# Sliding-window attention and a SiLU layer on one core: a planner is given later eviction times, and scores and values are placed by new gates

## The chip, the cores and the metric

The kernel runs on one core of one Trainium2 chip, in one launch. The metric is device microseconds of one execution. Six executions of the kernel before took 298.91 to 300.97 us, with a median of 299.58 us.

## The reference

The inputs are q, k and v of shape (8 batches, 8 heads, 576 positions, 64) and two weight matrices, all float32; the output is 4608 x 512 float32.

```python
scores = q @ k.T / 8                       # per batch and head, 576 x 576
mask   = (rel >= 0) & (rel < 64)           # rel = query position - key position
attn   = softmax(where(mask, scores, -1e9))
x      = (attn @ v), heads side by side    # 4608 rows, 512 columns
h      = x @ w_in                          # 512 -> 2048
out    = (h * sigmoid(h)) @ w_out          # 2048 -> 512
```

## The kernel before

**Two kinds of work.** Attention goes batch by batch, in units of three blocks of 64 positions: units (b, 0), (b, 1), (b, 2) for batch b. The dense part goes by tiles of 512 rows, tile 0 to tile 8. Tile b needs the attention of batches up to b. The program adds them in the order batch 0, tile 0, batch 1, tile 1, batch 2, and so on, so that the attention of batch b is meant to be mixed into tile b-1.

**A unit of attention** (from batch 1 on: all 8 heads). *Scores*: 48 small matmuls on a 32-row tiling of TensorE (line 331) into four PSUM banks at0 to at3. *Exponentials*: four on ScalarE (line 337), one per bank. *Masks*: four multiplications on VectorE (line 340). *Values*: 48 small matmuls on a 32-column tiling (line 349) into two banks. Then VectorE takes two reciprocals (356), two multiplications (359) and two transposes (363) into `bridge`, which the dense part reads.

**A dense tile.** First layer: 16 groups of four matmuls 128x512 (line 369), each group into one bank, then a SiLU on ScalarE from that bank (line 375). Second layer: four runs of 16 matmuls 128x512 (line 381), each run into one bank, then a copy (line 387) and a store. A tile from the second on has 64 matmuls in each layer (tile 1's first layer is cut finer; the last run of tile 8 is cut in three).

**Banks.** Eight PSUM banks: 0 to 3 are for scores (pool "at"), 4 to 7 for the dense part (pool "mp"); values take banks 4 and 5 (pool "pv").

**The planner.** Class `Plan` plays the whole program through with a cost for each operation, and the order that comes out is the order of the instructions on every engine. An engine that is free takes, of the operations at the heads of the queues of its classes, the one with the lowest `first` (rank of the class plus batch number), if its dependencies are `done`, its gate is open and its banks are idle. The values of batch b have rank 0 + b, scores 1 + b, a dense matmul 99, SiLU -3, copy-out -2, exponentials and masks 1 + b, reciprocals and the operations after them 0 + b, block transposes and shifts of later inputs 2 + b. An operation counts as done at `seen`, its end plus `lat`, by default 0.08. A bank is idle when the operation that empties it is done. Of idle banks, a dense operation takes first those that values don't use (6 and 7), and of these the one idle longest:

```python
idle.sort(key=lambda i: (op["pool"] == "mp" and i in self.pools["pv"],
                         max([u["seen"] for u in self.banks[i]], default=0.0)))
```

If an operation of another pool than "mp" is ready and only its banks are missing, its pool is kept for it (`kept`). ScalarE keeps one table loaded; a change between exponential and SiLU adds 1.28 in the plan.

The plan's costs, in its own microseconds: a dense matmul of 512 columns 0.0036 + 512/2400 = 0.217 (`lat` 0.1), SiLU of 512 columns 0.605, copy-out on ScalarE 0.621, scores 0.55, values 0.54, an exponential 0.39 (`lat` 0.2), a mask 0.37 (`lat` 0.2).

**Gates.** The list `moe` holds the dense matmuls in order, each with its kind (1: first layer, 2: second) and, for the second layer, `rest`: how many matmuls of the tile's second layer are left. `scores_may_run(whole)` (`whole` is true from batch 1 on) looks at the next dense matmul: scores run only in a second layer, while more than 14 matmuls are left. Values have no gate. Scores also depend on the masks of the unit ahead from batch 2 on (`g_mask[-1]`), on the transposed q and k (`kq_done`) and on the values of three units earlier (`old`).

Of the kernel before, what the change touches and what calls it, by code (L numbers as in the profile page):

```python
# [14 lines left out]
class Plan:  # L15
# [31 lines left out]
    def run(self):  # L47
        head = {c: 0 for c in self.queues}
        engines = sorted({e for q in self.queues.values() for op in q for e in op["us"]})
        free = {e: 0.0 for e in engines}  # L50
        can = {e: [c for c, q in self.queues.items() if any(e in op["us"] for op in q)] for e in engines}
        table, left = "exp", self.count
        pipe, sent = {True: 2.0, False: 0.0}, []
        events, order = [0.0], []
        while left:
            if not events:
                raise RuntimeError([(c, head[c], q[head[c]]["n"]) for c, q in self.queues.items() if head[c] < len(q)])
            now = self.now = heapq.heappop(events)
            while events and events[0] == now:
                heapq.heappop(events)  # L60
            moved = True
            while moved:
                moved = False
                for e in engines:
                    if free[e] > now:
                        continue
                    best, kept = None, set()
                    heads = [(self.queues[c][head[c]], c) for c in can[e] if head[c] < len(self.queues[c])]
                    for op, c in sorted(heads, key=lambda x: x[0]["first"]):
                        if e == "POOL" and op["dma"] and len(sent) >= 8 and sent[-8] > now:  # L70
                            continue
                        if e not in op["us"] or not self.done(op["deps"]) or (op["gate"] and not op["gate"]()):
                            continue
                        if op["pool"]:
                            idle = [i for i in self.pools[op["pool"]] if i not in kept and self.done(self.banks[i])]
                            if len(idle) < len(op["untils"]):
                                if op["pool"] != "mp":
                                    kept.update(self.pools[op["pool"]])
                                continue
                            idle.sort(key=lambda i: (op["pool"] == "mp" and i in self.pools["pv"],  # L80
                                                     max([u["seen"] for u in self.banks[i]], default=0.0)))
                            op["bank"] = idle[:len(op["untils"])]
                            for i, until in zip(op["bank"], op["untils"]):
                                self.banks[i] = until
                        best = (op, c)
                        break
                    if best is None:
                        continue
                    op, c = best
                    head[c] += 1  # L90
                    us = op["us"][e]
                    if op["table"] and op["table"] != table:
                        table, us = op["table"], us + 1.28
                    end = free[e] = now + us
                    soft = e == "POOL"
                    if op["dma"] is None:
                        op["seen"] = end + op["lat"]
                    elif soft:

                        begin = max(pipe[True], end + 1.4)  # L100
                        pipe[True] = begin + op["dma"] * (1.5 if pipe[False] > begin else 1.0)
                        op["seen"] = pipe[True] + op["lat"] + 1.2
                        sent.append(op["seen"])
                        heapq.heappush(events, op["seen"])
                    else:
                        begin = max(pipe[False], end + 1.0)
                        busy = pipe[True] > begin
                        pipe[False] = begin + op["dma"] * (1.6 if busy else 1.0)
                        if busy:
                            pipe[True] += 0.6 * op["dma"]  # L110
                        op["seen"] = pipe[False] + {"ld0": 1.2, "st": 1.2}.get(c, 3.0)
                    op["at"], op["cls"], op["by"] = now, c, e
                    order.append((op, e))
                    left -= c != "warm"
                    moved = True
                    heapq.heappush(events, end)
                    heapq.heappush(events, op["seen"])
        for op, e in order:
            op["fn"](e)
# [3 lines left out]
def kernel(ctx, tc, q, k, v, w_in, w_out, out):  # L123
# [275 lines left out]
    moe = []  # L399
    exps = {}  # L400

    def scores_may_run(whole):
        i = next((i for i in range(scores_may_run.i, len(moe)) if moe[i][0]["seen"] is None), None)
        if i is None:
            return True
        scores_may_run.i = i
        op, kind, rest = moe[i]
        if kind == 1:
            return not whole and rest > 0 and not p.done(op["deps"])
        return rest > (14 if whole else 6)  # L410
    scores_may_run.i = 0

    n_nat = [0, 0]
    def add_first_batch():
# [71 lines left out]
    def add_unit(b, g, which, n0):  # L486
        whole = b > 0
        first = "0" if b == 0 and g == 0 else ""
        na = len(which)
        ns = [n0 + i for i in range(na)]  # L490
        old = [d for n in ns for d in g_pv[n - NE // 2:n - NE // 2 + 1] * (n >= NE // 2)]
        s = p.add("s" + first, {"PE": 0.55 if b else 0.7}, None,
                  [d for a in which for d in kq_done[(b, a)]] + old + (g_mask[-1] if b > 1 else [] if b else c_bias),
                  lat=0.1, gate=lambda: scores_may_run(whole), pool="at" if b else "all", b=b, nb=2 * na)
        s["fn"] = lambda _: scores(s, b, g) if b else scores_first(s, which[0], g)
        s_last[b] = [s]
        ready = []
        for i in range(2 * na):
            ex = p.add("exp" + first, {"ACT": 0.39}, lambda _, i=i: expo(s["bank"][i], 2 * n0 + i), [s], lat=0.2, table="exp", b=b)
            s["untils"][i].append(ex)  # L500
            exps.setdefault(b, []).append(ex)
            if b:
                ex = p.add("mask", {"DVE": 0.37}, lambda _, i=i: masking(2 * n0 + i, g), [ex, *c_mask], b=b)
            ready.append(ex)
        g_mask.append(ready)
        pv = p.add("pv" + first, {"PE": 0.1 + 0.22 * na}, None, ready + [d for a in which for d in v_done[(b, a)]], lat=0.1,
                   pool="pv" if b > 1 or (b, g) > (1, 0) else "at" if b else "all", b=b, nb=na)

        def run_values(_):
            for i, a in enumerate(which):  # L510
                values(pv["bank"][i], b, a, g, ns[i])
        pv["fn"] = run_values
        pv_last[b] = [pv]
        for i, (n, a) in enumerate(zip(ns, which)):
            rc = p.add("inverse" + first, {"DVE": 0.21}, lambda _, i=i, n=n: inverse(pv["bank"][i], n),
                       [pv] + g_norm[n - NRC:n - NRC + 1] * (n >= NRC), b=b)
            no = p.add("norm" + first, {"DVE": 0.56}, lambda _, i=i, n=n: normal(pv["bank"][i], n),
                       [rc] + g_bridge[n - NOX:n - NOX + 1] * (n >= NOX), b=b)
            pv["untils"][i].append(no)
            g_norm.append(no)  # L520
            g_pv.append(pv)
            br = p.add("bridge" + first, {"DVE": 0.5}, lambda _, n=n, a=a: to_bridge(n, b, a, g), [no], b=b)
            g_bridge.append(br)
            o_done.setdefault(NG * b + g, []).append(br)

    n_gt, free_gt = [0], {}
    n_ot, free_ot = [0], {}
# [3 lines left out]
    def add_tile(j):  # L531
# [18 lines left out]
        for i, (ft, lo, hi) in enumerate(work):  # L550
# [3 lines left out]
            for c in range(NDC):  # L554
# [4 lines left out]
                op["fn"] = lambda _, bank=bank, ft=ft, c=c, lo=lo, hi=hi: first_layer(bank, j, ft, c, lo, hi)  # L559
                moe.append((op, 1, 1 if c == 0 and (i == 0 or hi > work[i - 1][2]) else -1))  # L560
            si.append(p.add("silu", {"ACT": 0.18 + (hi - lo) * 0.00083}, lambda _, bank=bank, g=g, lo=lo, hi=hi:
                            silu(bank, g, lo, hi), [op] + free_gt.get(g, []), table="silu"))
            bank["untils"][0] = [si[-1]]
        order = [(m, f, 0, d_model) for m in range(4) for f in range(NFT)]
        if j == 0:
# [4 lines left out]
        for i, (m, f, lo, hi) in enumerate(order):  # L570
# [7 lines left out]
            if f == NFT - 1:  # L578
# [1 line left out]
                n_ot[0] += 1  # L580
                cp = p.add("out", {"DVE": 0.18 + (hi - lo) / 1000, "ACT": 0.18 + (hi - lo) / 1160},
                           lambda e, bank=bank[(m, lo)], ot=ot, lo=lo, hi=hi: copy_out(e, bank, ot, lo, hi),
                           [op, free_ot.get(ot)])
                bank[(m, lo)]["untils"][0] = [cp]
                free_ot[ot] = p.add("st", {"SP": 0.45}, lambda _, ot=ot, m=m, lo=lo, hi=hi: store(ot, j, m, lo, hi), [cp],
                                    dma=0.75 * (hi - lo) / d_model)
# [65 lines left out]
```

The softmax here doesn't subtract the row's maximum and nothing guards it: scores larger than these inputs give would overflow.

## Time and profile before

| | |
|---|---|
| median of six executions | 299.58 us |
| lowest and highest | 298.91 and 300.97 us |
| profiled execution, its own time | 300.97 us |
| its span, first to last instruction | 299.2 us |
| TensorE (PE) busy | 290.7 us, 97% |
| ScalarE (ACT) busy | 176.3 us, 59% |
| VectorE (DVE) busy | 138.8 us, 46% |
| DMA-issuing GpSimd (POOL) | 117.5 us, 39% |
| granted TensorE clock, mean | 1.000 |

Times of the profile are microseconds from the start of the span. A row of the timeline names start, duration, engine, line, operation and count; what stands in brackets is the idle time of the engine before it and what ended that. The duration of one matmul includes the time through the array, so the distance between starts, not the duration, is what one matmul costs TensorE.

### The profile page before, as it was taken

The numbers are of one execution on the slowest core, as the hardware profiler recorded it, in microseconds if no ns is written. First come the engines' busy times: TensorE is split into PE (matmuls) and PEld (weight loads), VectorE is DVE, ScalarE is ACT, GpSimd is POOL, SyncE is SP. The second block draws the span as 40 slices with busy tenths as digits, with TensorE's granted clock in tenths as the row PEclk, the third lists the DMA queues.
The fourth block names the chain that finished last, engine by engine and source line by source line (L and its number), as shares of the span: only waits on it lengthen the run. The fifth ranks groups of instructions, "written<-read, shape, count | busy, mean of one in ns | idle before, by whom it ended". The sixth has DMA issues, their size and how long they took to land.

```text
span 299.2 us, 8516 instructions
## 1 busy us (share of the span) xinstructions
PE 290.7 (97%) x3641; PEld 149.4 (50%) x3641; DVE 138.8 (46%) x340; ACT 176.3 (59%) x340; POOL 117.5 (39%) x175
## 2 busy tenths in 40 slices
PE   7989989899999999999999999999999999999996
PEld 3556635785444544445444544445444544444444
DVE  3682467978886379337941693067006510000000
ACT  4778645886466745675378437752866376126511
POOL 8967976969799979870500000000000000000000
DMA  7999999999999999992860110011001100110012
GB/s 156 175 202 169 148 174 149 228 135 134 172 172 143 112 184 168 154 96 74 82 71 0 72 39 36 2 37 72 35 0 39 72 35 0 37 71 35 2 70 71
DMA packets 82982, 28.64 MB, mean 96 GB/s; under 512 B 72448, under 2 KB 78208, under 8 KB 82944
## 3 DMA queue, kind: packets, MB, share of 16 engines
q0 software_dynamic: 77184, 18.07, 65.5%
q1 hardware_dynamic: 5760, 10.03, 9.4%
q8 instruction: 28, 0.46, 0.7%
q14 instruction: 10, 0.08, 0.1%
HBM read 36.70 MB, written 9.44 MB: 154 GB/s over the span
## 4 chain that ended last, share of the span: by engine, by line
PE 83%; DMA 8%; POOL 6%; issue 1%; ACT 1%; POOLq 0%; ACTq 0%
PE mp L381 40%; PE mp L369 37%; PE at L331 3%; PE mp L349 3%; DMA w_in_sb<-in_moe_w_in_dram 3%; DMA w_out_sb<-in_moe_w_out_dram 2%; DMA vv<-in_v_dram 2%; POOL nat L239 2%; POOL vv L253 2%; POOL natb L229 1%; POOL w_out_sb L265 1%; POOL w_in_sb L259 0%; ACT ot L387 0%; ACT g L375 0%; PE at L349 0%
## 5 line engine op out<-in xcount | busy, mean ns | idle before, releaser
L381 PE MATMUL mp<-w_out_sb,g 128*128 128x512 bf16 (+2 forms) x608 | 130.1, 368 | 1.3 <-DMA w_out_sb<-in_moe_w_out_dram 1.3
L369 PE MATMUL mp<-bridge,w_in_sb 128*128 128x512 bf16 (+5 forms) x696 | 128.9, 342 | 1.6 <-ACT g L375 1.0
L375 ACT ACTIVATE g<-mp 128x512 bf16<-128x512 f32 (+5 forms) x174 | 89.5, 523 | 31.1 <-PE mp L369 29.9
L369 PEld LDWEIGHTS <-w_in_sb 128*128 128x128 bf16 x696 | 66.3, 97 | 62.5 <-issue 7.6
L381 PEld LDWEIGHTS <-g 128*128 128x128 bf16 x608 | 55.9, 98 | 62.6 <-issue 2.0
L387 ACT COPY ot<-mp 128x512 f32<-128x512 f32 (+2 forms) x36 | 20.2, 563 | 62.1 <-PE mp L381 46.2
L340 DVE TENSOR_TENSOR e<-e,mask 128x384 bf16<-128x384 bf16 x84 | 26.0, 347 | 49.3 <-ACT e L337 48.8
L337 ACT ACTIVATE e<-at 128x384 bf16<-128x384 f32 x90 | 37.3, 497 | 16.2 <-PE at L331 15.9
L239 POOL DMA_DIRECT2D nat<-in_k_dram x56 | 34.7, 637 | 11.3 <-DMA vv<-in_v_dram 6.2
L253 POOL DMA_DIRECT2D vv<-in_v_dram x32 | 32.0, 1022 | 12.9 <-PE mp L349 12.5
L239 POOL DMA_DIRECT2D nat<-in_q_dram x56 | 34.8, 641 | 4.0 <-DMA vv<-in_v_dram 1.1
L363 DVE STREAM_TRANSPOSE bridge<-ox 128x384 bf16<-128x384 bf16 x48 | 24.7, 551 | 0.0
L246 DVE STREAM_TRANSPOSE kt<-nat 128x576 bf16<-128x576 bf16 x28 | 20.7, 780 | 6.2 <-DMA nat<-in_k_dram 6.2
L246 DVE STREAM_TRANSPOSE qt<-nat 128x576 bf16<-128x576 bf16 x28 | 20.8, 786 | 3.5 <-DMA nat<-in_q_dram 3.4
L359 DVE TENSOR_TENSOR ox<-mp,rc 128x384 bf16<-128x384 f32 x43 | 21.4, 536 | 0.1
L356 DVE RECIPROCAL rc<-mp 128x6 f32<-128x6 f32 x43 | 7.9, 190 | 18.8 <-PE mp L349 18.0
L349 PEld LDWEIGHTS <-e 128*32 128x32 bf16 x1152 | 10.9, 95 | 9.6 <-issue 5.9
L299 DVE COPY vv<-vv 64x576 bf16<-64x576 bf16 (+1 forms) x14 | 7.4, 530 | 14.2 <-DMA vv<-in_v_dram 11.8
L349 PE MATMUL mp<-vv,e 128*32 128x65 bf16 x1032 | 12.7, 194 | 0.7 <-issue 0.7
L331 PE MATMUL at<-qt,kt 32*128 32x64 bf16 x1008 | 11.6, 190 | 0.0
L331 PEld LDWEIGHTS <-kt 32*128 32x128 bf16 x1008 | 9.3, 92 | 4.3 <-issue 3.3
L337 ACT ACT_TABLE_LOAD x7 | 9.0, 1283 | 0.1
(53 smaller groups left out, 84.7 us busy)
## 6 DMA issues: line engine op xcount, KB each, us to landing
out_dram<-ot SPq DMA_DIRECT2D x35, 256.0 KB, 2.2
vv<-in_v_dram POOLq DMA_DIRECT2D x32, 144.0 KB, 5.4
nat<-in_q_dram POOLq DMA_DIRECT2D x56, 72.0 KB, 4.0
nat<-in_k_dram POOLq DMA_DIRECT2D x56, 72.0 KB, 3.9
w_out_sb<-in_moe_w_out_dram POOLq DMA_DIRECT2D x8, 256.0 KB, 7.0
w_in_sb<-in_moe_w_in_dram POOLq DMA_DIRECT2D x6, 256.0 KB, 7.6
w_in_sb<-in_moe_w_in_dram POOLq DMA_DIRECT2D x4, 128.0 KB, 6.2
natb<-in_q_dram POOLq DMA_DIRECT2D x3, 144.0 KB, 5.9
```

The costliest lines, as they stand in the source:

```text
L239: nc.gpsimd.dma_start(out=nats[i][32 * h:32 * h + 32].rearrange("p (m x) -> p m x", m=NB), in_=(q, k)[kk][b, 4 * a + h].rearrange("(m p r) ...
L246: nc.vector.transpose(out=to[:, (2 * a + part) * S:(2 * a + part + 1) * S].rearrange("x (m t r) -> x m r t", t=32, r=2), in_=nats[i].rearr ...
L253: queue[e].dma_start(out=vv[b % NV][:, 2 * g0 + 1:2 * g1 + 1:2, 0:D], in_=v[b].rearrange("h s d -> (h s) d").rearrange("(g p) d -> p g d", ...
L331: nc.tensor.matmul(at_six(op["bank"][h])[:, a, x], lhsT=kt[b % NK][r, at:at + 128], rhs=qt[b % NK][r, at:at + 64], start=(s == a == x == 0 ...
L337: nc.scalar.activation(out=es[n % NE], in_=at_six(bank), func=ACTF.Exp, scale=scale)
L340: nc.vector.tensor_mul(es[n % NE], es[n % NE], mask0 if g == 0 else mask)
L349: nc.tensor.matmul(at_pv(bank)[32 * h:32 * h + 32, x, t], lhsT=e_of(b, a, n, h)[:, x, 32 * t:32 * t + 32], rhs=vv[b % NV][:, (4 * a + h) * ...
L359: nc.vector.tensor_mul(oxs[n % NOX], at_pv(bank)[:, :, :, 0:D], rcs[n % NRC].unsqueeze(3).to_broadcast([128, 3, 2, D]))
L363: nc.vector.transpose(out=bridge[:, n0:n0 + 3, 2 * a:2 * a + 2].rearrange("x t s (u i) -> x t s u i", u=2), in_=oxs[n % NOX].rearrange("p ...
L369: nc.tensor.matmul(banks[bank["bank"][0]][:, 0:hi - lo], lhsT=w_in_sb[:, c, ft * 128:(ft + 1) * 128], rhs=bridge[:, (j * TT + lo) // 64:(j ...
L375: nc.scalar.activation(out=gts[gt][:, lo:hi], in_=banks[bank["bank"][0]][:, 0:hi - lo], func=ACTF.Silu)
L381: nc.tensor.matmul(banks[bank["bank"][0]][:, 0:hi - lo], lhsT=gts[gt][:, m * 128:(m + 1) * 128], rhs=w_out_sb[:, f, lo:hi], start=(f == 0) ...
```

## The change

Four edits.

1. The `lat` of a SiLU and of a copy-out goes from 0.08 to 0.22 in tiles from the third on (`j > 1`), so that the plan takes their banks to be idle 0.14 later.
2. When all values are placed, the dense part may use all eight banks.
3. Values from batch 2 on get a gate, `values_may_run`: they run when the next scores could run too, or when fewer than five matmuls of the second layer are left, or when the next dense matmul isn't ready, or when no scores are left.
4. Scores from batch 3 on don't run while values are ready and waiting (`values_wait`), and the first scores of a batch (`g == 0`, from batch 3 on) need only more than 3 matmuls left in the second layer, where the others need more than 14.

```diff
                         if op["pool"]:
-                            idle = [i for i in self.pools[op["pool"]] if i not in kept and self.done(self.banks[i])]
+                            idle = [i for i in self.pools[op["pool"] if head["pv"] < len(self.queues["pv"]) else "all"] if i not in kept and self.done(self.banks[i])]
...
-    def scores_may_run(whole):
+    def scores_may_run(whole, more):
...
         if kind == 1:
             return not whole and rest > 0 and not p.done(op["deps"])
-        return rest > (14 if whole else 6)
+        return rest > (more if whole else 6)
     scores_may_run.i = 0
+
+    def next_of(ops):
+        return next((op for op in ops if op["seen"] is None), None)
+
+    def values_wait(b):
+        pv = next_of(p.queues["pv"])
+        return b > 2 and pv is not None and p.done(pv["deps"])
+
+    def values_may_run():
+        s, op = next_of(p.queues["s"]), next_of(op for op, _, _ in moe[scores_may_run.i:])
+        if s is None or op is None or not p.done(op["deps"]):
+            return True
+        kind, rest = next((kind, rest) for o, kind, rest in moe[scores_may_run.i:] if o is op)
+        return kind == 2 and rest < 5 or p.done(s["deps"]) and scores_may_run(True, s["more"])
...
+        more = 3 if b > 2 and g == 0 else 14
         s = p.add("s" + first, {"PE": 0.55 if b else 0.7}, None,
...
-                  lat=0.1, gate=lambda: scores_may_run(whole), pool="at" if b else "all", b=b, nb=2 * na)
+                  lat=0.1, gate=lambda: scores_may_run(whole, more) and not values_wait(b), pool="at" if b else "all", b=b, nb=2 * na)
+        s["more"] = more
...
         pv = p.add("pv" + first, {"PE": 0.1 + 0.22 * na}, None, ready + [d for a in which for d in v_done[(b, a)]], lat=0.1,
+                   gate=values_may_run if b > 1 else None,
...
             si.append(p.add("silu", {"ACT": 0.18 + (hi - lo) * 0.00083}, lambda _, bank=bank, g=g, lo=lo, hi=hi:
-                            silu(bank, g, lo, hi), [op] + free_gt.get(g, []), table="silu"))
+                            silu(bank, g, lo, hi), [op] + free_gt.get(g, []), lat=0.22 if j > 1 else 0.08, table="silu"))
...
-                           [op, free_ot.get(ot)])
+                           [op, free_ot.get(ot)], lat=0.22 if j > 1 else 0.08)
```

## The prediction

> **What bounds the kernel now.** I read the page's busy times first, then TensorE's timeline, then the chain that ended last, then ScalarE's timeline in a first layer, then the windows.
>
> ```profile
> PE 290.7 (97%) x3641; PEld 149.4 (50%) x3641; DVE 138.8 (46%) x340; ACT 176.3 (59%) x340; POOL 117.5 (39%) x175
> ```
>
> TensorE is busy 290.7 of 299.2 us. A gain must come out of its own stream: fewer interruptions, or the few tens of nanoseconds that a busy share doesn't show. Tile 5's second layer on TensorE, from the timeline:
>
> ```profile
> 192.18 0.55 PE L331 MATMUL at<-qt,kt 32*128 32x64 bf16 x48
> 192.66 4.06 PE L381 MATMUL mp<-w_out_sb,g 128*128 128x512 bf16 x18
> 196.65 0.56 PE L349 MATMUL mp<-vv,e 128*32 128x65 bf16 x48
> 197.14 0.55 PE L331 MATMUL at<-qt,kt 32*128 32x64 bf16 x48
> 197.62 4.06 PE L381 MATMUL mp<-w_out_sb,g 128*128 128x512 bf16 x18
> ...
> 206.57 0.56 PE L349 MATMUL mp<-vv,e 128*32 128x65 bf16 x48
> 207.06 2.33 PE L381 MATMUL mp<-w_out_sb,g 128*128 128x512 bf16 x10
> 209.23 14.16 PE L369 MATMUL mp<-bridge,w_in_sb 128*128 128x512 bf16 x64
> 223.32 0.55 PE L331 MATMUL at<-qt,kt 32*128 32x64 bf16 x48
> ```
>
> The pattern of a tile is: scores alone, 18 matmuls, values and scores together, 18, values and scores, 18, values alone, 10, then 64 of the first layer. Tiles 2 to 6 all read so; tile 1 has 21, 21, 21 and 1. The chain's end shows the two layers without attention:
>
> ```profile
> 240.54 14.00 PE mp L369 x64
> 254.53 13.81 PE mp L381 x64
> 268.35 14.08 PE mp L369 x64
> ```
>
> Both layers have 64 matmuls of 512 columns, yet the first takes 0.19 and 0.27 us more. ScalarE's timeline in tile 7's first layer says why:
>
> ```profile
> 247.55 0.60 ACT L375 ACTIVATE g<-mp 128x512 bf16<-128x512 f32 x1 [0.27 <-PE mp L369]
> 248.42 0.60 ACT L375 ACTIVATE g<-mp 128x512 bf16<-128x512 f32 x1 [0.27 <-PE mp L369]
> 249.32 0.60 ACT L375 ACTIVATE g<-mp 128x512 bf16<-128x512 f32 x1 [0.31 <-PE mp L369]
> 250.19 0.60 ACT L375 ACTIVATE g<-mp 128x512 bf16<-128x512 f32 x1 [0.27 <-PE mp L369]
> 251.09 0.60 ACT L375 ACTIVATE g<-mp 128x512 bf16<-128x512 f32 x1 [0.31 <-PE mp L369]
> ```
>
> ScalarE waits for TensorE before each SiLU, so it isn't the bound; but from 248 us on, every second group comes 0.90 instead of 0.87 after the one before. In the plan, ScalarE that has caught up starts a SiLU 0.1 after its group's end; the bank is seen idle at 0.1 + 0.605 + 0.08 = 0.785, before the next-but-one group at 4 x 0.217 = 0.868. So the plan swings between banks 6 and 7 only. On the chip the bank comes back later: its return ends the period of the delayed group, 0.863 (13.81/16) plus some 0.044, so about 0.907 after the group's end. Every second group stalls TensorE for 0.044 us, since the stall itself gives the other bank time. While ScalarE lags (table load, then four SiLUs in a row) the plan itself goes on to banks 4 and 5, and no stall shows.
>
> **Edit 1, banks by later eviction times.** With `lat` 0.22 the bank is seen idle at 0.925, after 0.868; the plan must take a third bank (4 or 5) every third group, and a bank then has two groups' time, 1.73 us on the chip against the 0.907 it needs. The rotation ends the stall. Worth: tile 7 0.19, tile 8 0.27; in tiles 2 to 6 a first layer lasts 14.09 (209.23 to 223.32), of which 0.095 is the switch to small tiles worked out below, so 0.185 over 13.81. Sum 5 x 0.185 + 0.19 + 0.27 = **1.39 us**, all on the path, as TensorE never waits for data there. Bounds: nothing (the plan finds no third bank) to 1.39. I take the whole: the nearest row is tile 1's first layer, which already rotates over three or four banks (shorter SiLUs against shorter groups), and whose long run shows no such stall. SiLUs, copies and stores issue the same DMAs on SP; nothing is queued anew.
>
> The page "TensorE: Matmul & The Clock Gate", section "A second HAM failure mode: psum-queue depth-cycling", speaks against this edit: by it, 512-column matmuls that cycle through banks leave micro-idles that make the clock fall to half and recover. By that rule one of the page's windows of 3.4 us at half clock would cost 1.7 us, an estimate from that page alone, and the sum would be no gain. The windows of the trace stand against it here, PEclk being the third number from the end:
>
> ```profile
> 84.62:98.70 14.08, 14.08 (x65) 6.12 (x63) 9.84 (x16) 10.61 (x17) 13.48 (x20) 1.00 1.65 145
> 268.18:282.26 14.08, 14.08 (x65) 6.19 (x64) 0.00 (x0) 9.54 (x16) 0.00 (x0) 1.00 0.05 19
> ```
>
> The clock is 1.00 in both, the first over its early groups on four banks, the second on two with the stalls.
>
> **Edit 2, all banks after the last values.** It touches tiles 7 and 8 and the end of 6; there it makes the third bank certain. No further gain; its part is in the 1.39.
>
> **Edits 3 and 4, where scores and values stand.** What a place costs: 64 second-layer matmuls take 13.81, 0.2158 each, so 18 take 3.885; from 192.66 to 196.65 they take 3.99. The 0.105 over is the turn to the small tiling at the end (about 0.095) and the restart (about 0.01). Scores cost 0.48 (192.18 to 192.66) and values 0.49 whether a dense matmul or scores follow (206.57 to 207.06, 196.65 to 197.14). Values and scores side by side therefore save one 0.105.
>
> How many pairs come about, by the plan. Tile 1 stays: values (2, 2) come at 1 left, and fewer than five open the gate. Tile 2: scores at 64, pairs at 46 and 28, values (3, 2) at 10; the next scores (4, 0) now need only more than 3, their q and k are transposed in tile 2's first layer, so they go beside: a pair gained. The values (4, 0) become ready in tile 3's first layer and wait there some 10 us for the second. Behind them on TensorE nothing waits, for the plan puts first-layer matmuls there instead; their reader is tile 4's first layer, 27 us on; the masked `es` buffers and rows they hold are asked for three units later. Tile 3: pair (values (4, 0), scores (4, 1)) at 64, pairs at 46 and 28, the last with scores (5, 0). Values (5, 0) are ready at about 10, or 7 if two block transposes (1.49 us in the trace) fall between; scores (5, 1) need more than 14, so the values wait until fewer than five and go alone. From there each tile has scores alone, two pairs, values alone, as now. In all 13 pairs against 12: **0.11 us**. Bounds: nothing, and at most 17 pairs of 18 units, five more, 0.53 us, if the values of a tile's end are ready too late for the second layer, wait over each first layer and find the next scores.
>
> What the moves cost. Four exponentials (0.38 apart) of scores (4, 0) run beside tile 2's last 10 matmuls (2.17 us), no table load before them; ScalarE then has its first SiLU 0.86 us later: nothing. Without that cover, see the slow rival. Four masks (0.36 each) go into a first layer where VectorE is busy 10 of 14 us: nothing. Values alone with four matmuls left hold banks 4 and 5 for about 1.8 us; the first layer asks for its third bank some 0.9 + 1.7 us after the values' end: nothing, at worst 0.05 in each of three tiles. Batch 7's v load, which waits for values (4, 2), is issued about 4 us earlier on POOL; the queue is empty by then, and its reader is tens of microseconds off.
>
> **The sum.** 1.39 + 0.11 = 1.50 us off the span: 299.2 to 297.7. The profiled execution's own time is 1.77 above its span, 300.97, and would be 299.5; the median of the runs stands 1.39 under that execution, so 299.58 - 1.50 = **298.1 us**. The case's own range, 0.9 to 1.92 off (half of the bank gain, or all pairs) and a few tenths for the runs' own spread, is 297.4 to 298.7.
>
> **The rivals.**
> *The bank edit doesn't bite.* The plan's margin is small: 0.925 against 0.868. Should banks 4 and 5 be kept for values whose gate is open, or the release order still favour 6 and 7, the stalls stay, and 0.11 is left: 299.5. For it: 0.057 of margin. Against: the gate holds values shut through a first layer, so nothing keeps 4 and 5.
> *Slower: tables change to and fro.* If scores run so late in a second layer that a SiLU is ready before the fourth exponential, the SiLU has the lower rank; ScalarE loads its table (1.283 us), and a later gap takes the exponential: 1.283 + 0.38 + 1.283 = 2.95. The next SiLU is 2.95 - 0.27 = 2.68 late; four banks carry three more groups, 2.59; TensorE stalls 0.907 + 2.68 - 2.59 = 1.0 us. At five borders (tiles 2-3 to 6-7) that is 5.0, less 1.5: 303.1. It decides from two borders on. Point of onset: the fourth exponential starts 0.65 + 3 x 0.39 = 1.82 after the scores' start, the first SiLU is ready at 1.52 + 0.217 for each matmul left, so it needs at most one left; the gate asks for over 3. A table load before the exponentials would move that to seven left. Against: no SiLU stands between scores of one second layer.
> *Held values everywhere.* The bound of 17 pairs, 1.92 off: 297.7. It lies in the forecast's range.
>
> **How the numbers follow.** Forecast with the held-values case: 0.72. Bank edit without effect, or most of it eaten: 0.15. Slower by table changes or another wait that the later values bring: 0.13. A measurement of this kernel can tell about 0.3%, 0.9 us, from no change: faster is below 298.7, which the forecast fills; same 0.15, slower 0.13. The range that leaves out 2 in 10 is 297.2 to 299.5: the forecast's own, its runs' spread, and the near part of the second case.
>
> **What the changed profile would show.** First layers of tiles 2 to 8 at 13.8 to 13.9 us for 64 matmuls (13.99 with the switch), and no 0.90 step between SiLUs; else edit 1 is wrong. In tile 2's second layer values and scores side by side with 10 left, then 64 first-layer matmuls, then values and scores again; in tiles 3 to 5 values alone with four left. Seven exponential and seven SiLU table loads; more speak for the slow rival. PEclk 1.00 throughout. A new idle gap of TensorE ahead of line 349 or 369 would make the forecast wrong.

## The result, and the profile after

The changed kernel takes 298.35 us in the median (297.27 to 299.65, 25 runs) against 299.71 us of the kernel before (51 runs). The ratio is 0.9953, with a 95% interval of 0.9941 to 0.9965: 1.41 us less, between 1.05 and 1.77.

The page's busy times of the changed kernel, and from its groups of instructions the table loads (operation and count, then busy time and mean ns of one):

```profile
span 296.7 us, 8534 instructions
PE 288.8 (97%) x3641; PEld 150.0 (51%) x3641; DVE 138.2 (47%) x340; ACT 176.0 (59%) x340; POOL 117.9 (40%) x175
```

```profile
L337 ACT ACT_TABLE_LOAD x7 | 9.0, 1283 | 0.1
L375 ACT ACT_TABLE_LOAD x7 | 9.0, 1283 | 0.1
```

The share of TensorE is the same 97% although the kernel is shorter: the stalls of 0.044 us that went were counted as busy (the window 268.18 to 282.26 of the kernel before, shown with the prediction, holds six of them and has TensorE busy for 14.08 of 14.08 us). The table loads are the seven and seven of before.

The span fell by 2.5 us, from 299.2 to 296.7, but not all of it is the change. Tile 2's first layer begins at 84.63 in the execution before and at 83.77 after, and up to there the two programs have the same order on TensorE. The 0.86 us lies in waits for loads, which differ between executions; the largest is a wait of TensorE for `w_out` in tile 0's second layer, 1.3 us in the execution before and none after. From the first matmul of tile 2's first layer to the last matmul of the program the profiled executions take 211.47 us before (84.627 to 296.101) and 209.84 after (83.773 to 293.617). This **stretch** is 1.63 us shorter; it is used below to compare profiles.

TensorE's timeline around tiles 2 and 3 of the changed kernel:

```profile
112.07 0.56 PE L349 MATMUL mp<-vv,e 128*32 128x65 bf16 x48
112.56 0.57 PE L331 MATMUL at<-qt,kt 32*128 32x64 bf16 x48
113.06 2.33 PE L381 MATMUL mp<-w_out_sb,g 128*128 128x512 bf16 x10
115.23 13.98 PE L369 MATMUL mp<-bridge,w_in_sb 128*128 128x512 bf16 x64
129.05 1.24 PE L381 MATMUL mp<-w_out_sb,g 128*128 128x512 bf16 x5
130.22 0.56 PE L349 MATMUL mp<-vv,e 128*32 128x65 bf16 x48
130.71 0.55 PE L331 MATMUL at<-qt,kt 32*128 32x64 bf16 x48
131.19 4.49 PE L381 MATMUL mp<-w_out_sb,g 128*128 128x512 bf16 x20
135.61 0.56 PE L349 MATMUL mp<-vv,e 128*32 128x65 bf16 x48
136.10 0.57 PE L331 MATMUL at<-qt,kt 32*128 32x64 bf16 x48
136.61 4.06 PE L381 MATMUL mp<-w_out_sb,g 128*128 128x512 bf16 x18
140.60 0.56 PE L349 MATMUL mp<-vv,e 128*32 128x65 bf16 x48
141.09 0.57 PE L331 MATMUL at<-qt,kt 32*128 32x64 bf16 x48
141.59 4.71 PE L381 MATMUL mp<-w_out_sb,g 128*128 128x512 bf16 x21
146.13 13.98 PE L369 MATMUL mp<-bridge,w_in_sb 128*128 128x512 bf16 x64
```

The first rows are values (3, 2) beside scores (4, 0), with 10 matmuls left in tile 2, as foretold. Values (4, 0) wait through the whole first layer (115.23 to 129.05), but then five more matmuls come before them; the next stretch is 20 matmuls rather than 18; and after scores (5, 0) the second layer ends with 21 matmuls and no values alone. So values (5, 0) wait over the next first layer too. Tiles 2 to 5 all have three pairs; in all there are 15 pairs (values directly followed by scores), where 13 were foretold and 12 stood before.

ScalarE's timeline in tile 7's first layer, and the windows of the first layers of tiles 7 and 8:

```profile
247.23 0.60 ACT L375 ACTIVATE g<-mp 128x512 bf16<-128x512 f32 x1 [0.27 <-PE mp L369]
248.10 0.60 ACT L375 ACTIVATE g<-mp 128x512 bf16<-128x512 f32 x1 [0.27 <-PE mp L369]
248.96 0.60 ACT L375 ACTIVATE g<-at 128x512 bf16<-128x512 f32 x1 [0.27 <-PE at L369]
249.82 0.60 ACT L375 ACTIVATE g<-at 128x512 bf16<-128x512 f32 x1 [0.27 <-PE at L369]
```

```profile
238.34:252.15 13.81, 13.81 (x65) 6.23 (x64) 0.00 (x0) 10.61 (x17) 0.00 (x0) 1.00 0.06 21
265.97:279.78 13.81, 13.81 (x65) 6.27 (x64) 0.00 (x0) 9.54 (x16) 0.00 (x0) 1.00 0.06 20
```

Every SiLU now comes 0.86 or 0.87 after the one before; the 0.90 steps are gone. TensorE's own starts say the same for all the tiles: in the first layers of tiles 2 to 8 the kernel before has 30 steps of 0.26 us from one matmul to the next where nearly all the others are 0.216, four in each tile and six in tile 8, always eight matmuls (two groups) apart; the changed kernel has no step over 0.22. Both first layers take 13.81 us, just what 64 second-layer matmuls take, where they took 14.00 and 14.08. The granted clock is 1.00.

### The profile page after: what moved, and what is told of

The parts are those of the page before. It is cut to its first block, busy times and chain, and to the rows that moved or that the text cites. A ratio compares the mean times of both kernels' runs of the same rounds, so it can differ in the third digit from the quotient of the medians.

```text
span 296.7 us, 8534 instructions
## 1 busy us (share of the span) xinstructions
PE 288.8 (97%) x3641; PEld 150.0 (51%) x3641; DVE 138.2 (47%) x340; ACT 176.0 (59%) x340; POOL 117.9 (40%) x175
## 4 chain that ended last, share of the span: by engine, by line
PE 94%; DMA 2%; ACT 2%; issue 1%; ACTq 0%; POOLq 0%
PE mp L369 36%; PE mp L381 34%; PE at L381 8%; PE at L369 6%; PE at L331 3%; PE mp L349 3%; DMA natb<-in_q_dram 2%; PE at L311 0%; ACT ot L387 0%; ACT g L375 0%; PE at L282 0%; PE mp L282 0%; ACT L623 0%; PE mp L311 0%; PE at L319 0%
## 5 line engine op out<-in xcount | busy, mean ns | idle before, releaser
L369 PE MATMUL mp<-bridge,w_in_sb 128*128 128x512 bf16 (+5 forms) x612 | 109.9, 337 | 2.0 <-ACT g L375 0.8
L381 PE MATMUL mp<-w_out_sb,g 128*128 128x512 bf16 (+2 forms) x480 | 104.8, 371 | 0.0
L375 ACT ACTIVATE g<-mp 128x512 bf16<-128x512 f32 (+5 forms) x153 | 77.0, 513 | 24.9 <-PE mp L369 23.5
L337 ACT ACTIVATE e<-at 128x384 bf16<-128x384 f32 x90 | 38.0, 496 | 24.8 <-PE at L331 24.3
L340 DVE TENSOR_TENSOR e<-e,mask 128x384 bf16<-128x384 bf16 x84 | 25.4, 345 | 23.9 <-ACT e L337 23.7
L387 ACT COPY ot<-mp 128x512 f32<-128x512 f32 (+2 forms) x28 | 15.8, 568 | 32.9 <-issue 16.2
L381 PE MATMUL at<-w_out_sb,g 128*128 128x512 bf16 (+1 forms) x128 | 25.7, 359 | 0.0
L369 PE MATMUL at<-bridge,w_in_sb 128*128 128x512 bf16 x84 | 19.3, 379 | 0.0
L387 ACT COPY ot<-at 128x512 f32<-128x512 f32 (+1 forms) x8 | 4.4, 545 | 20.7 <-PE at L381 20.7
L375 ACT ACTIVATE g<-at 128x512 bf16<-128x512 f32 x21 | 12.3, 597 | 4.8 <-PE at L369 4.8
```

The costliest lines, as they stand in the source:

```text
L337: nc.scalar.activation(out=es[n % NE], in_=at_six(bank), func=ACTF.Exp, scale=scale)
L340: nc.vector.tensor_mul(es[n % NE], es[n % NE], mask0 if g == 0 else mask)
L369: nc.tensor.matmul(banks[bank["bank"][0]][:, 0:hi - lo], lhsT=w_in_sb[:, c, ft * 128:(ft + 1) * 128], rhs=bridge[:, (j * TT + lo) // 64:(j ...
L375: nc.scalar.activation(out=gts[gt][:, lo:hi], in_=banks[bank["bank"][0]][:, 0:hi - lo], func=ACTF.Silu)
L381: nc.tensor.matmul(banks[bank["bank"][0]][:, 0:hi - lo], lhsT=gts[gt][:, m * 128:(m + 1) * 128], rhs=w_out_sb[:, f, lo:hi], start=(f == 0) ...
L387: copies[e](out=ots[ot][:, lo:hi], in_=banks[bank["bank"][0]][:, 0:hi - lo])
```

## The experiments

All are compared with the kernel before on the same chip. The stretch is worked out from the starts in each profile. Pairs are counted in the order of instructions that each kernel's plan makes, since a few matmul records are missing from the traces. The theory: edit 1 is worth 1.35 us through a third bank, and each pair of values and scores about 0.1 us. The rivals: the gates carry the gain, or the later eviction time works otherwise than through banks. For e7 and e9 there is one run each; they are compared by the stretch, not by the time.

| run | median us (before) | ratio, 95% interval | stretch us | pairs |
|---|---|---|---|---|
| before | 299.71 | 1 | 211.47 | 12 |
| changed kernel | 298.35 (299.71) | 0.9953 (0.9941 to 0.9965) | 209.84 | 15 |
| e1 edit 1 alone | 298.95 (299.81) | 0.9958 (0.9937 to 0.9980) | 210.13 | 12 |
| e2 gates alone | 299.98 (299.81) | 1.0002 (0.9981 to 1.0022) | 211.41 | 13 |
| e3 never side by side | 300.00 (299.81) | 0.9999 (0.9979 to 1.0020) | 211.78 | 0 |
| e4 rotation, no `lat` | 298.71 (299.81) | 0.9959 (0.9936 to 0.9982) | 210.14 | 12 |
| e5 `lat` 0.15 | 299.55 (299.71) | 0.9992 (0.9976 to 1.0008) | 211.39 | 12 |
| e6 `lat` 0.17 | 298.50 (299.71) | 0.9963 (0.9949 to 0.9978) | 210.13 | 12 |
| e7 without edit 2 | 297.75, one run | none | 209.84 | 15 |
| e8 more banks, held | 297.09 (299.71) | 0.9927 (0.9908 to 0.9945) | 210.22 | 17 |
| e9 last groups on 6, 7 | 299.94, one run | none | 210.25 | 13 |
| e10 six banks, held | 297.38 (299.78) | 0.9930 (0.9903 to 0.9957) | 210.26 | 17 |

**e1, edit 1 alone.** The kernel before with `lat=0.22 if j > 1 else 0.08` at the SiLU and the copy-out, and nothing else.

> Edit 1 alone on the kernel before (eviction seen 0.22 after its end from tile 2 on), no new gates. If the two-bank swing is what stalls TensorE: first layers of tiles 2 to 8 at 13.81 us for 64 matmuls, 12 pairs of values and scores as before, 1.35 us less than before, ratio 0.9955. If the gain of the whole change is in the placing of values and scores: no change, ratio 1.000.

The stretch is 1.35 us shorter and the ratio 0.9958; the order on TensorE is that of before, and no step over 0.22 us is left within the first layers. Edit 1 carries most of the gain without any gate.

**e2, the gates alone.** The changed kernel with edits 1 and 2 taken back:

```diff
-... self.pools[op["pool"] if head["pv"] < len(self.queues["pv"]) else "all"] ...
+... self.pools[op["pool"]] ...
-... lat=0.22 if j > 1 else 0.08 ...      (SiLU and copy-out)
```

> Edits 3 and 4 alone, evictions seen at 0.08 and banks as before. By the price of 0.105 us for a pair: 13 pairs against 12, so 0.1 us less, ratio 0.9997, with the 0.044 us stalls still in the first layers (14.0 us). If the gates carry the gain: 1 us or more less, ratio 0.996.

No change in the runs, and 0.07 us in the stretch (0.067 before rounding), for one pair more. The price of 0.105 isn't reached because the bursts of scores of this profile take 0.04 us more in all (four last 0.57 us where most last 0.55; in the kernel before two do); why some do isn't known. TensorE's timeline of tile 3 in this run:

```profile
115.19 14.16 PE L369 MATMUL mp<-bridge,w_in_sb 128*128 128x512 bf16 x64
129.28 0.56 PE L349 MATMUL mp<-vv,e 128*32 128x65 bf16 x48
129.77 0.55 PE L331 MATMUL at<-qt,kt 32*128 32x64 bf16 x48
...
146.22 0.81 PE L381 MATMUL mp<-w_out_sb,g 128*128 128x512 bf16 x3 [0.16 <-issue]
```

Without edit 1 the first layer keeps its stalls (129.28 - 115.19 = 14.09), and the held values stand at the very start of the second layer, as the prediction had them; values alone go ahead of the last four matmuls (one record is missing of the four, hence the idle time shown).

**e3, never side by side.** The changed kernel with one more condition on scores:

```diff
+    pv_at = [None]
+    def apart():
+        i = next((i for i in range(scores_may_run.i, len(moe)) if moe[i][0]["seen"] is None), len(moe))
+        done = sum(op["seen"] is not None for op in p.queues["pv"])
+        if pv_at[0] is None or pv_at[0][0] != done:
+            pv_at[0] = (done, i)
+        return done < 6 or i > pv_at[0][1]
...
-    gate=lambda: scores_may_run(whole, more) and not values_wait(b)
+    gate=lambda: scores_may_run(whole, more) and not values_wait(b) and apart()
```

> The changed kernel with one more gate: scores wait for one dense matmul after values, so that no pair is left of 15. By 0.105 us for a pair: 1.6 us more than the changed kernel, 0.2 us more than before, ratio about 1.0005. If a pair is worth nothing, because TensorE makes up for the turns elsewhere: as the changed kernel, ratio 0.9953.

The kernel is back at the time of before. TensorE's timeline of tile 3:

```profile
129.68 0.56 PE L349 MATMUL mp<-vv,e 128*32 128x65 bf16 x48
130.49 0.55 PE L331 MATMUL at<-qt,kt 32*128 32x64 bf16 x48 [0.25 <-issue]
```

Scores start 0.81 us after values, where they start 0.49 after them in a pair: the dense matmul between them (0.216, its record is missing, hence the idle time shown) and one more turn (0.105) make the difference of 0.32. In the stretch it takes 1.94 us more than the changed kernel, of which 0.60 is one unit of values (0.49 and its turn of 0.105) that has moved from tile 1 into the stretch; the other 1.34, over the 13 pairs that the changed kernel has in the stretch, makes 0.103 us for a pair. From tile 1's first matmul to the last of the program, where all 15 pairs lie and no unit moves in or out, it takes 243.38 us against 241.79: 1.59 more, as expected, or 0.106 for a pair. The price from the profile before was 0.105.

**e4, another way to a third bank.** The kernel before; the first layer from tile 2 on takes the bank idle longest of all four:

```diff
+        {..., "mp": range(4, 8), "mp1": range(4, 8), ...}
-                           pool=None if c else "mp")
+                           pool=None if c else "mp1" if j > 1 else "mp")
```

> The kernel before, with the first layer of tiles from the third on taking the bank idle longest of 4 to 7 (no preference for 6 and 7), evictions seen at 0.08, order of operations as before. If the bank is the cause: as edit 1 alone, 1.35 us less, ratio 0.9955. If the later eviction time works otherwise (through the order of copies, stores or SiLUs): no change, ratio 1.000.

ScalarE's timeline in tile 7:

```profile
247.07 0.60 ACT L375 ACTIVATE g<-mp 128x512 bf16<-128x512 f32 x1 [0.27 <-PE mp L369]
247.93 0.60 ACT L375 ACTIVATE g<-mp 128x512 bf16<-128x512 f32 x1 [0.27 <-PE mp L369]
248.80 0.60 ACT L375 ACTIVATE g<-mp 128x512 bf16<-128x512 f32 x1 [0.27 <-PE mp L369]
```

The 0.90 step is gone and the stretch is 1.34 us shorter, as in e1, with the eviction time left at 0.08 and the order of operations on every engine that of before. So the gain is that of the bank chosen, not of anything else that the later time does.

**e5 and e6, the two sides of the plan's threshold.** Edit 1 alone with 0.15 and with 0.17 in place of 0.22.

> Edit 1 alone with 0.15 in place of 0.22: in the plan 0.1 + 0.605 + 0.15 = 0.855, before the group's 0.868. By the bank theory the plan still swings between two banks and nothing is gained: ratio 1.000, stalls of 0.044 us in the first layers. If the gain grows steadily with the eviction time: about 0.5 of the way from 0.08 to 0.22, 0.7 us less, ratio 0.9977.

> Edit 1 alone with 0.17: in the plan 0.875, just after 0.868. By the bank theory the whole gain is there: 1.35 us less, ratio 0.9955, no stalls. If the gain grows steadily with the eviction time: 0.9 us less, ratio 0.997.

ScalarE's timeline in tile 7, first of e5, then of e6:

```profile
247.49 0.60 ACT L375 ACTIVATE g<-mp 128x512 bf16<-128x512 f32 x1 [0.27 <-PE mp L369]
248.40 0.60 ACT L375 ACTIVATE g<-mp 128x512 bf16<-128x512 f32 x1 [0.31 <-PE mp L369]
249.26 0.60 ACT L375 ACTIVATE g<-mp 128x512 bf16<-128x512 f32 x1 [0.27 <-PE mp L369]
```

```profile
247.86 0.60 ACT L375 ACTIVATE g<-mp 128x512 bf16<-128x512 f32 x1 [0.27 <-PE mp L369]
248.72 0.60 ACT L375 ACTIVATE g<-mp 128x512 bf16<-128x512 f32 x1 [0.27 <-PE mp L369]
249.59 0.60 ACT L375 ACTIVATE g<-mp 128x512 bf16<-128x512 f32 x1 [0.27 <-PE mp L369]
```

At 0.15 the long step is there (247.49 to 248.40, 0.91), at 0.17 it isn't. The stretch goes from 211.39 to 210.13 between the two: 1.26 us for 0.02 in a number of the planner. e5 is itself 0.09 us shorter than before (0.087 before rounding), which fits the copy-out's part: in the plan of before the second group of a first layer, from tile 3 on, takes the bank that the last copy-out has just left, and in e5's plan another. On TensorE the fifth matmul of these six first layers starts 0.233 us after the fourth in before, and 0.216 after it in e5: 0.10 us in all. The copy-out's `lat` was not run by itself.

**e7, without edit 2.**

```diff
-... self.pools[op["pool"] if head["pv"] < len(self.queues["pv"]) else "all"] ...
+... self.pools[op["pool"]] ...
```

> The changed kernel without edit 2 (all banks after the last values). As the third bank comes from the later eviction time: first layers of tiles 7 and 8 at 13.81 us as in the changed kernel. If edit 2 is what frees the last two tiles: 14.0 and 14.08 us there.

```profile
237.61:251.42 13.81, 13.81 (x65) 6.24 (x64) 0.00 (x0) 10.58 (x17) 0.00 (x0) 1.00 0.06 21
265.24:279.05 13.81, 13.81 (x66) 6.27 (x64) 0.00 (x0) 9.54 (x16) 0.00 (x0) 1.00 0.05 20
```

The windows of the first layers of tiles 7 and 8, and the stretch, are those of the changed kernel to 0.01 us. Edit 2 brings nothing measurable here.

**e8 and e10, versions that go further.** Both are the changed kernel with values always held for the next scores, and with banks 0 to 3 opened to the start of tile 1's first layer (e8), or banks 0 to 3, 6 and 7 (e10):

```diff
-        return kind == 2 and rest < 5 or p.done(s["deps"]) and scores_may_run(True, s["more"])
+        return p.done(s["deps"]) and scores_may_run(True, s["more"])
...
+        {..., "low": range(4), ...}                             # e10: [0, 1, 2, 3, 6, 7]
-                           pool=None if c else "mp")
+                           pool=None if c else "low" if j == 1 and i < 8 else "mp")    # e10: i < 14
```

> The changed kernel with two more edits: the first 8 groups of tile 1's first layer take banks 0 to 3, which hold nothing then, and values are always held for the next scores (17 pairs for 15). In the changed kernel TensorE stops four times, 1.5 us in all, between 51.8 and 57.1 us, where the four copies of tile 0 and the values hold banks 4 to 7. By the bank theory: 1.3 us there and 0.2 us for two pairs less than the changed kernel, ratio to before about 0.990. If tile 1's start waits for the values of batch 1 rather than for banks: 0.2 us less than the changed kernel, ratio 0.9946.

> The changed kernel with values always held for the next scores and the first 14 groups of tile 1's first layer on banks 0 to 3, 6 and 7 (eight groups on banks 0 to 3 alone in the run before, whose TensorE still stopped 0.66 us there). If those last stops are banks: 0.5 us less than that run, ratio to before about 0.991. If ScalarE, which empties the banks, sets the pace there: as that run, 0.9927.

e8 has the lowest ratio, 0.9927 of before (2.2 us less), about 0.8 us below the changed kernel by the ratios, whose intervals just overlap, and not the 1.5 us expected. e10 is no better. From tile 1's first layer to the last matmul both take 241.02 us; the changed kernel, from the same place in its order (51.64, before the stall that opens its tile 1), takes 241.98: 0.96 less for both. The two pairs account for 0.2 (the stretch of e8 holds values (2, 2), moved from tile 1 as in e3; without their 0.60 it is 209.62 against 209.84), the banks of tile 1 for the other 0.74; that is a subtraction, the two edits were not run apart. TensorE's and VectorE's timelines of e10 show what took the rest:

```profile
55.16 0.56 PE L349 MATMUL mp<-vv,e 128*32 128x65 bf16 x48
...
57.51 8.02 PE L369 MATMUL mp<-bridge,w_in_sb 128*128 128x256 bf16 x64 [0.36 <-ACT g L375]
```

```profile
55.62 0.45 DVE L356 RECIPROCAL rc<-mp 128x6 f32<-128x6 f32 x2 [0.33 <-PE mp L349]
55.98 0.98 DVE L359 TENSOR_TENSOR ox<-mp,rc 128x384 bf16<-128x384 f32 x2
56.88 1.03 DVE L363 STREAM_TRANSPOSE bridge<-ox 128x384 bf16<-128x384 bf16 x2
```

The first half of the tile's columns is done early now, and the second half needs `bridge` of values (1, 2). The two transposes end at 57.45 and 57.91, and TensorE's next matmuls start at 57.51 and then, after a second stop, at 57.96, 0.06 and 0.05 after those ends. The stop is labelled with ScalarE, but ScalarE's SiLUs ahead of it end at 57.18 and 57.51 and its next starts at 58.37, so the second stop at least can't be theirs. Neither of the two theories for e10 holds: not banks and not ScalarE, but the chain from the values through VectorE, is next there.

**e9, what makes 15 pairs of 13.** The changed kernel, but from tile 3 on the last two groups of a first layer take banks 6 and 7 only:

```diff
+        {..., "end": range(6, 8), ...}
-                           pool=None if c else "mp")
+                           pool=None if c else "end" if j > 2 and ft > 13 else "mp")
```

> The changed kernel, but from tile 3 on the last two groups of a first layer may take banks 6 and 7 only. If the held values start five matmuls into the second layer of tile 3 because the last group sits in bank 4, and if those five are what makes 15 pairs out of 13: values and scores stand right at the start of tile 3's second layer, then 18, 18, and values alone near its end; 13 pairs, and from tile 2's first layer to the last matmul 0.2 us for two pairs and some 0.2 us for stalls of the last group (0.04 each) more than the changed kernel's 209.84 us. If the later start has another cause: five matmuls first and 15 pairs as in the changed kernel.

```profile
116.27 14.02 PE L369 MATMUL mp<-bridge,w_in_sb 128*128 128x512 bf16 x64
130.22 0.56 PE L349 MATMUL mp<-vv,e 128*32 128x65 bf16 x48
130.71 0.55 PE L331 MATMUL at<-qt,kt 32*128 32x64 bf16 x48
...
146.44 0.56 PE L349 MATMUL mp<-vv,e 128*32 128x65 bf16 x48
147.15 0.81 PE L381 MATMUL mp<-w_out_sb,g 128*128 128x512 bf16 x3 [0.16 <-issue]
```

The held values stand at the start of the second layer, and values (5, 0) go alone near its end (again one record of four is missing): 13 pairs, and 0.41 us more than the changed kernel, as expected to 0.01 us. So the banks of the last first-layer groups decide how many pairs there are.

## Why the prediction was right

The forecast was 298.1 us and 1.50 us off; measured are 298.35 us, 1.41 off by the ratio, with 1.50 inside its interval. The stretch, which leaves out the waits for loads, shows 1.63 off. So the mechanism of the large term was right, and the closeness of the sum is in part luck: the banks gave 0.04 less than foretold and the pairs 0.17 more.

- **Edit 1**: foretold 1.39, measured 1.35 (e1); the terms of 0.185 for tiles 2 to 6 were read from tile 5 and are 0.17 to 0.185 in the five. The mechanism stood: two banks in turn, a bank that the plan took as free too early, and a third bank as cure (e4, e5, e6). Taking tile 1's first layer as the nearest row was right.
- **Edit 2**: foretold nothing of its own; measured nothing (e7).
- **The price of a pair**: foretold 0.105, measured 0.103 to 0.106 (e3).
- **The count of pairs**: foretold 13, measured 15. This step failed. The prediction put values (4, 0) and scores (4, 1) at 64 left and values (5, 0) alone at the end, and that is the order which edits 3 and 4 give by themselves (e2). It overlooked that edit 1 acts on them: the last first-layer group sits in bank 4, which values need; with the later eviction time the plan lets five matmuls go first, and the whole tile slides by five (e9 shows this). The plan is an ordinary program: played through with both edits it gives bank 4, the five matmuls and the 15 pairs, so the count need not have been worked out by hand. The next interval is 20 instead of 18; in the plan a copy-out then goes between the exponentials, which was read from the order, not tried. Values (5, 0) come too late for the second layer and are held, so tiles 3 to 5 keep three pairs. The sign that the prediction named for its count, values alone with four left in tiles 3 to 5, fails in tiles 3 and 4; tile 5 ends with values alone and three left. The term was 0.11 and measures 0.28 (209.84 against 210.13 in e1); the bound of 0.53 held it.
- **The range's upper end**: the prediction calls 0.9 off "half of the bank gain", but half of 1.39 and the one pair make 0.8. The measured gain is clear of both.
- **The moves' costs**: foretold at nothing. The table loads stayed seven and seven, no new stop of TensorE shows in the stretch, and the first layers take 13.81 us beside the added masks. The slow rival's alternation of tables didn't come up.
- **The rival without effect** would have been true for the stalls with a `lat` of 0.15 (e5: 0.855 in the plan, before 0.868). At 0.22 the margin of 0.925 against 0.868 held, as the prediction argued.
- **The rule against the edit** that the prediction took from the Trainium skill (page "TensorE: Matmul & The Clock Gate", section "A second HAM failure mode: psum-queue depth-cycling"), bank cycling that lets the clock fall, isn't seen here: the clock is 1.00 in the first layers of tiles 7 and 8, which rotate over more banks than before.

## What to carry to other kernels

A busy share of 97% can hide a regular stall: compare the starts of equal work in two stages (here 64 matmuls in 13.81 and 14.08 us), and look for a step that comes every second time. Where an order is planned with costs, a resource that the plan frees too early (here at 0.785 us, against some 0.907 on the chip) is taken again too early every time, and the gain of correcting it comes all at once at a threshold. Two edits to one planner aren't a sum: work out the order with both, or let the planner play it through, since one of them may move what the other counts.

## What was not expected of the hardware

The same order of TensorE gives the same time to about 0.01 us over 210 us: the stretch is 209.84 us in the changed kernel and in e7, on different executions, and 210.13 in e1 and e6. The spread between executions, 297.27 to 299.65 us for the changed kernel, lies for the profiles seen here ahead of the stretch, in the part that waits for loads. And a wait of some 0.04 us costs TensorE 0.04 us but shows in no list of waits: between 240 and 283 us the kernel before has ten of them, and the list of TensorE's waits there is empty. The row of a 512-column matmul lasts 0.38 us and the next starts 0.22 or 0.26 after it, so the rows overlap either way; only the spacing of starts shows the wait.
